# An interleaved state-space and feed-forward kernel: weight scales, a convolution step and a spectrum put elsewhere in a hand-ordered stretch

## The chip, the cores and the metric

The kernel runs on one core of a Trainium2 chip. A core has TensorE (PE in the profile), with a second queue for loading its weights (PEld), VectorE (DVE), ScalarE (ACT), GpSimd (POOL) and SyncE (SP), which here only issues transfers. Each engine works through its own list of instructions in order; engines wait for each other by semaphores. The metric is the device time of one execution, in microseconds (us).

## What is computed

Two rounds of two layers on a sequence `x` of 2048 rows and 512 channels: a state-space convolution and a gated feed-forward part, each behind a layer norm and with a residual. The core of the reference:

```python
dt = jnp.exp(log_dt)[:, None]
logdA, dB = dt * (A_re + 1j * A_im), dt * (B_re + 1j * B_im)
P = jnp.exp(logdA[:, :, None] * l[None, None, :])      # l = 0 .. 2047, 128 states
K = jnp.einsum("dn,dnl,dn->dl", Cc, P, dB).real
Kf, Uf = rfft2(pad(K)), rfft2(pad(u.T))
y = irfft2(Uf * Kf)[..., :L].T + u * Dskip

x = A_u
x = x + A_ref(layernorm(x), ...)      # the convolution above
x = x + B_ref(layernorm(x), ...)      # (silu(x @ w_gate) * (x @ w_up)) @ w_down, 1376 wide
x = x + A_ref(layernorm(x), ...)
x = x + B_ref(layernorm(x), ...)
```

Both rounds use the same weights and the same kernel `K`.

## The kernel before

**Tiling.** The sequence is cut into four blocks of 512 rows. The convolution is done block by block with short Fourier transforms, written as matmuls: the 512 rows fall into residues, called `q`, taken in the order 0, 3, 1, 2 (`QORD`), and the channels into two halves `h` of 256. A block's spectra are products of a DFT matrix with its normed rows (`direct`, L288 to L300, in fp32, to a DRAM buffer `udr`). One *step* of a convolution (`ssm_half`, L738) belongs to one `h` and `q`: for each of the blocks up to this one a product of its spectrum with the matching piece of the kernel's spectrum (L781; `w0r` stays in on-chip memory and serves the block itself, `wdr` holds the pieces for earlier blocks in DRAM), a sum (L784), two instructions that make the complex result `yf` (L786 and L787), and then the inverse transform on TensorE (L803, result `pi`) that ACT or DVE joins to sums and differences `bb` (L753, L761, L762). After the four steps of an `h`, some sixteen small instructions (from L818) add the outcome to the rows.

**Stages.** For the first 250 us or so the kernel's spectrum is generated in eight chunks of channels (`lags`, L496 and L497, then spectra, L531, L580). Weights are meanwhile loaded only to find their maxima, `cmx` (L339). From the maxima `scales` (L342 to L356, eleven tiny DVE instructions) makes powers of two, `sc`. With these each weight is split into a high half on ACT (L664) and a low half on DVE (L669), both fp16, `wsl`. From about 326 us the rest runs: (layer, block) in the order of `SEQ` = (0,0), (0,1), (0,2), (1,0), (0,3), (1,1), (1,2), (1,3), a feed-forward part for each (`ffn`: L916 to L919 into `pgu`, `sg` on ACT and DVE, L931 to L933 into `py`, the residual at L936), with the next block's convolution woven in.

**What lies between: the handoff**, about 250 to 326 us, is what the change touches. On PE, DVE, ACT and POOL it is written out by hand: within `manual_schedule` the order of the calls in the source is the order of the engines. `take(g, n)` runs the generator `g` through `n` of its yields; `split(hi, lo, load)` issues so many high halves, low halves and loads of weights. The work there is the eighth chunk's lags and spectra (`first_parts` L580, `later_parts` L531, with `wos` L598 to L600), block 0's convolution in two halves `conv[0]` and `conv[1]` (its spectra lie in `u4`, part of the tile `mix`, which is loaded again for the second half), the splitting of the first weights, block 0's second norm `norm` (statistics L203 to L209, `nn` L848, transposes L850, then L853 and L855 into `mix`), and the first steps of block 1's convolution, `block1`. `direct_size` (L187) takes the largest skip weight: `da` on ACT (L192), one row of 512, and `dmax` on DVE (L193). SP's list is ordered by a scheduler, and its transfers wait there in that order, each for its buffer.

**Buffers that matter.** Tile `uu` has three buffers, two of which hold the normed rows of block 1's neighbour whose last spectra are still to be taken (L296, `n`); `w` has three, `hf` and `y1` one, and there are four small accumulators (`pi`, `pw`, `pf`).

## Time and profile before

| | us |
|---|---|
| median of 3 runs | 1154.03 |
| lowest, highest | 1152.23, 1155.5 |
| the profiled execution | 1154.49 |
| its span | 1152.7 |
| PE busy in it | 1099.8 (95%) |
| DVE busy | 998.9 (87%) |
| ACT busy | 599.1 (52%) |
| POOL busy | 108.7 (9%) |

The profile is of one execution. Its views give groups of instructions by line and engine, the idle time before them with what ended it, the waits summed by line and by what was waited for, and a timeline. A row like `wsl<-st,sc` reads output from inputs; `[5.16 <-ACT wsl L664]` behind it says that the engine was idle for 5.16 us, until ACT's write of `wsl` at line 664. A transfer's time runs from its issue to its landing.

Line numbers are those of the kernel before. In the changed kernel the lines of `ssm_half` and what follows are others: L775 is the inverse transform (L803 before), L803 the product (L781), L806 the sum (L784), L808 and L809 make `yf` (L786, L787), L759 and L760 the `bb` on DVE (L761, L762), L751 the `bb` on ACT (L753), L864, L866, L869, L871 the norm's (L848, L850, L853, L855), L932, L933, L935 the gate and up products (L916, L917, L919), L939 `sg` (L923).

### The profile page before, as it was taken

The page shows a single profiled execution, that of the slowest core. Times are in us where ns is not written, and L with a number is a line of the kernel's source. Part 1 is how long each engine was busy: PE and PEld are TensorE (multiplying, and loading weights), DVE is VectorE, ACT ScalarE, POOL GpSimd, SP SyncE. Part 2 cuts the span into 40 slices and gives each one's busy share as a digit, 9 for nine tenths or more (in the row PEclk, how much of TensorE's full clock was granted, in tenths as well). Part 3 has the DMA queues.
Part 4 walks back from the last instruction along what each step waited for, and adds up shares of the span by engine and source line. Part 5 has one row for each costly group of instructions (what it writes and reads, how often), then busy time and mean ns, then how long its engine had stood idle before and what let it go on. Part 6 is the DMA issues. An engine that isn't in the chain of part 4 may idle for free.

```text
span 1152.7 us, 24401 instructions
## 1 busy us (share of the span) xinstructions
PE 1099.8 (95%) x9942; PEld 877.3 (76%) x9942; DVE 998.9 (87%) x1585; ACT 599.1 (52%) x1198; POOL 108.7 (9%) x163
## 2 busy tenths in 40 slices
PE   2989999998899999999999999999999999999998
PEld 1868888887876868686868687877778687876874
DVE  8999999988999899998999999989994999973211
ACT  6989889733554453567453534655434352334211
POOL 0112222210000010011010000110000100000000
PEclk9989999998999999999999999999999999999999
DMA  5367677867583355322353444333443155302000
GB/s 210 129 164 166 162 186 170 194 184 250 172 263 109 106 152 192 114 97 71 110 144 130 131 142 151 108 118 110 143 132 130 50 134 156 102 32 48 14 24 19
DMA packets 127314, 150.38 MB, mean 130 GB/s; under 512 B 50897, under 2 KB 75985, under 8 KB 127202
## 3 DMA queue, kind: packets, MB, share of 16 engines
q1 hardware_dynamic: 115298, 123.32, 34.6%
q0 software_dynamic: 11904, 25.50, 9.5%
q8 instruction: 78, 1.28, 0.5%
q14 instruction: 34, 0.28, 0.1%
HBM read 98.70 MB, written 33.82 MB: 115 GB/s over the span
## 4 chain that ended last, share of the span: by engine, by line
PE 40%; DVE 21%; issue 7%; ACT 3%; DMA 3%; POOL 1%; SPq 1%; DVEq 0%; ACTq 0%; POOLq 0%
PE pgu L916 7%; PE pgu L917 7%; PE pgu L919 7%; PE py L931 4%; PE py L932 4%; PE py L933 4%; PE pi L803 4%; DVE t L781 3%; DVE yk L784 3%; PE pf L280 2%; DVE z L228 2%; DVE yk L781 2%; DMA mix<-nn 1%; DVE sg L923 1%; DVE hl L925 1%
## 5 line engine op out<-in xcount | busy, mean ns | idle before, releaser
L916 PE MATMUL pgu<-mix,wsl 128*128 128x256 f16 x1280 | 299.4, 273 | 4.1 <-DVE sg L923 2.9
L917 PE MATMUL pgu<-mix,wsl 128*128 128x256 f16 x1280 | 299.1, 273 | 0.0
L919 PE MATMUL pgu<-mix,wsl 128*128 128x256 f16 x1280 | 195.6, 273 | 0.0
L917 PEld LDWEIGHTS <-wsl 128*128 128x128 f16 x1280 | 125.5, 98 | 20.9 <-issue 4.6
L931 PE MATMUL py<-wsl,hh 128*128 128x512 f16 (+1 forms) x352 | 133.4, 379 | 4.8 <-DVE xg L936 3.2
L916 PEld LDWEIGHTS <-wsl 128*128 128x128 f16 x1280 | 125.4, 98 | 16.1
L919 PEld LDWEIGHTS <-wsl 128*128 128x128 f16 x1280 | 125.6, 98 | 15.2
L933 PE MATMUL py<-wsl,hl 128*128 128x512 f16 (+1 forms) x352 | 133.4, 379 | 0.1
L922 ACT ACTIVATE sg<-pgu,sc 128x512 f32<-128x512 f32 x80 | 54.6, 683 | 128.4 <-PE pgu L919 126.6
L932 PE MATMUL py<-wsl,hh 128*128 128x512 f16 x320 | 121.3, 379 | 0.0
L781 DVE TENSOR_TENSOR t<-uu,w 128x1024 f32<-128x1024 f32 x96 | 116.8, 1216 | 0.2
L784 DVE TENSOR_TENSOR yk<-yk,t 128x1024 f32<-128x1024 f32 x96 | 116.7, 1216 | 0.2
L923 DVE SCALAR_TENSOR_TENSOR sg<-pgu,sc,sg 128x512 f32<-128x512 f32 x80 | 59.6, 745 | 52.6 <-ACT sg L922 52.3
L531 PE MATMUL pw<-kt,ek 128*128 128x256 f32 (+1 forms) x384 | 92.8, 380 | 0.0
L924 ACT ACTIVATE hh<-sg 128x512 f16<-128x512 f32 x80 | 50.1, 627 | 78.2 <-DVE sg L923 78.2
L531 PEld LDWEIGHTS pw<-kt,ek 128*128 128x128 f32 x384 | 74.3, 198 | 8.7
L803 PE MATMUL pi<-yl,mix 128*128 128x256 f16 x576 | 78.9, 273 | 1.2 <-ACT yl L792 0.8
L280 PE MATMUL pf<-z,eh 128*128 128x256 f16 x576 | 74.9, 273 | 0.6 <-DVE z L228 0.6
L781 DVE TENSOR_TENSOR yk<-u,w0r 128x1024 f32<-128x1024 f32 x56 | 68.1, 1216 | 0.8 <-ACT u L282 0.8
L925 DVE TENSOR_TENSOR hl<-sg,hh 128x512 f16<-128x512 f32 x80 | 54.8, 685 | 15.6 <-ACT hh L924 15.4
L496 PE MATMUL pk<-re,g 128*32 128x64 f32 x1024 | 65.1, 317 | 1.9 <-DMA g<-g 1.2
L932 PEld LDWEIGHTS <-hh 128*128 128x128 f16 (+1 forms) x352 | 34.5, 98 | 41.7 <-issue 5.9
(238 smaller groups left out, 2158.8 us busy)
## 6 DMA issues: line engine op xcount, KB each, us to landing
uu<-udr SPq DMA_DIRECT2D x96, 256.0 KB, 3.0
w<-wdr SPq DMA_DIRECT2D x96, 256.0 KB, 2.7
udr<-u POOLq DMA_DIRECT2D x32, 256.0 KB, 2.7
g<-g POOLq DMA_DIRECT2D x6, 1024.0 KB, 9.0
udr<-u SPq DMA_DIRECT2D x16, 256.0 KB, 2.9
n<-xdr SPq DMA_DIRECT2D x4, 1024.0 KB, 5.7
kdr<-ks SPq DMA_DIRECT2D x6, 512.0 KB, 2.6
kt<-kdr SPq DMA_DIRECT2D x24, 128.0 KB, 3.0
```

What stands on the lines that cost most here:

```text
L280: PE.matmul(pf[:, o], lhsT=e, rhs=m, start=k == 0, stop=k == len(terms) - 1)
L531: PE.matmul(pw[:, i], lhsT=e, rhs=kt[:, :, c + 4 * k0:4 * k1:4, :].rearrange("p g k d -> p k g d"), start=c == 0, stop=c == 3)
L781: V.tensor_tensor(t, uu.unsqueeze(2).to_broadcast([P, NQ, 2, 2, DC]), w.unsqueeze(3).to_broadcast([P, NQ, 2, 2, DC]), OP.mult)
L784: V.tensor_tensor(yk, yk, t, OP.add)
L803: PE.matmul(pi[:, o], lhsT=e, rhs=m, start=k == 0, stop=k == len(terms) - 1)
L916: PE.matmul(o, lhsT=wgu(wi, k, 0)[:, fs], rhs=nh[:, k], start=k == 0, stop=False)
L917: PE.matmul(o, lhsT=wgu(wi, k, 1)[:, fs], rhs=nh[:, k], start=False, stop=False)
L919: PE.matmul(o, lhsT=wgu(wi, k, 0)[:, fs], rhs=nlo[:, k], start=False, stop=k == 3)
L923: V.scalar_tensor_tensor(sg, pgu[:, 1], sc6[:, 4:5], sg, OP.mult, OP.mult)
L931: PE.matmul(py[:, r], lhsT=hh[:n, f, rc], rhs=wd(f, 0)[:n], start=f == 0, stop=False)
L932: PE.matmul(py[:, r], lhsT=hh[:n, f, rc], rhs=wd(f, 1)[:n], start=False, stop=False)
L933: PE.matmul(py[:, r], lhsT=hl[:n, f, rc], rhs=wd(f, 0)[:n], start=False, stop=f == FT - 1)
```

## The change

Three groups of steps change their place in the handoff; what is computed is the same.

1. The last weight maxima, the scales and the first high half stand right behind the eighth chunk's lags, ahead of everything of block 0's convolution. Its low half and a load follow sooner.
2. Block 1's first step (up to `yf`, without its inverse transform) stands ahead of block 0's second half, and with it `direct_size`; the second step stands where the first stood. Their inverse transforms are issued later, from a list (`made`, `inverse`). The first step's `u` is loaded in `ssm_half` itself, and its `yf` goes to a buffer of `w`.
3. The last spectrum of the second block (`second(*sec[-1])`: PE at L296, ACT at L299, a transfer to `udr`) stands ahead of the norm's transposes, in place of the end of the handoff; two of `later_parts`'s steps (`odd`) follow sooner too.

```diff
@@ inputs
+                        elif h + i == 0:
+                            continue
@@ ssm_half
-        if (layer, b) == SEQ[1] and not yf2:
-            t = tl([P, 2, 2, HD], "yf2", "hf")
-            yf2.extend((t[:, 0], t[:, 1]))
...
-        late = []
+        late, made = [], []
+        ahead_two = (layer, b, h) == (0, 1, 0)
+
+        def inverse(q, y, yl):
...
         for s in range(4):
-            hq, q, u = ahead.pop(0)
-            nxt = next(spec, None)
-            if nxt:
-                ahead.append(nxt)
+            if ahead_two and s == 0:
+                q, u = QORD[0], tl([P, NQ, 2, DC], "u", "u")
+                nc.sync.dma_start(u, udr[0][1, 0, q])
+            else:
+                hq, q, u = ahead.pop(0)
...
-            y = yc if half else yf2[s % 2] if (layer, b) == SEQ[1] else tl([P, 2, HD], "yf", "w")
+            if (layer, b, h + s > 0) == (*SEQ[1], True) and not yf2:
+                t = tl([P, 2, 2, HD], "yf2", "hf")
+                yf2.extend((t[:, 0], t[:, 1]))
+            y = yc if half else yf2[s % 2] if (layer, b, h + s > 0) == (*SEQ[1], True) else tl([P, 2, HD], "yf", "w")
...
-            if (layer, b, h, s) == (0, 1, 0, 0):
-                yield
...
+            made.append((q, y, yl))
+            if ahead_two and s == 0:
+                yield
+                continue
+            while made:
+                if ahead_two and s == 1:
+                    yield
+                inverse(*made.pop(0))
             yield
@@ weights: the last group's maxima are left for the handoff
-                    t0, t1, t2, t3 = 15.0, 20.0, 24.0, 27.0
+                    t0, t1, t2, t3 = 15.0, 20.0, 24.0, None
@@ the handoff
+        while tops:
+            tops.pop(0)()
+        scales()
+        split(1, 0)
         ks = spread_in(pk)
...
+        last = second(*sec[-1])
         norm = first_norm(tl([P, 2, D], "nn1", "hf"))
         take(conv[0], 1)
         spread_pe(ks, kts[1])
         skip(c, kts[1], G)
+        split(0, 1)
+        split(0, 0, 1)
         take(conv[0], 1)
-        scales()
-        split(1, 0)
         first_parts(c, 0)
         take(conv[0], 1)
-        split(1, 1)
-        split(0, 0, 1)
+        split(1, 0)
         first_parts(c - 1, 3)
         split(1, 0)
         take(conv[0], 1)
         first_parts(c - 1, 1)
         split(1, 0)
+        direct_size()
+        block1 = ssm(0, 1)
+        take(block1, 1)
+        split(0, 1)
+        split(0, 0, 1)
         take(conv[1], 1)
         first_parts(c, 2)
         take(conv[1], 1)
-        split(0, 1)
-        split(0, 0, 1)
...
-        direct_size()
-        block1 = ssm(0, 1)
         take(norm, 1)
         take(rest, 2)
         take(odd, 1)
+        take(last, 1)
+        take(odd, 2)
         take(norm, 1)
+        take(last, 1)
         take(block1, 1)
         take(rest, 1)
-        take(odd, 2)
         split(1, 0)
...
-        take(second(*sec[-1]), 2)
```

**DVE, from block 0's fourth step on, before.** `mix,w0r` are products of block 0, `u,w0r` and `uu,w` those of block 1.

```order
L781 TENSOR_TENSOR yk<-mix,w0r 128x1024
L786 TENSOR_TENSOR yf<-yk 128x256
L787 TENSOR_TENSOR yf<-yk 128x256
L761 TENSOR_TENSOR bb<-bb,pi 128x512
L762 TENSOR_TENSOR bb<-bb,pi 128x512
L781 TENSOR_TENSOR yk<-mix,w0r 128x1024
L786 TENSOR_TENSOR yf<-yk 128x256
L787 TENSOR_TENSOR yf<-yk 128x256
```

The same place now:

```order
L759 TENSOR_TENSOR bb<-bb,pi 128x512
L760 TENSOR_TENSOR bb<-bb,pi 128x512
L193 TENSOR_REDUCE dmax<-da 1x1
L803 TENSOR_TENSOR yk<-u,w0r 128x1024
L803 TENSOR_TENSOR t<-uu,w 128x1024
L806 TENSOR_TENSOR yk<-yk,t 128x1024
L808 TENSOR_TENSOR yf<-yk 128x256
L809 TENSOR_TENSOR yf<-yk 128x256
L669 SCALAR_TENSOR_TENSOR wsl_2666<-wsl_2667,sc_92,wsl_2665 128x4x344
L803 TENSOR_TENSOR yk<-mix,w0r 128x1024
```

`dmax`, the five instructions of block 1's first step and a low half stand between block 0's first `bb` pair and its fifth step.

**ACT, from the eighth chunk's lags on, before.** `ks<-pk` (L507) copies the lags.

```order
L507 ACTIVATE ks<-pk 128x1024
L753 ACTIVATE bb<-pi 128x512
L525 ACTIVATE kt_429<-kp 128x1024
L664 ACTIVATE wsl_2665<-st_2533,sc_92 128x4x344
L581 ACTIVATE w0r<-pw 128x128
L753 ACTIVATE bb<-pi 128x512
L664 ACTIVATE wsl_2666<-wsl_2668,sc_92 128x4x344
L581 ACTIVATE w0r<-pw 128x2x2x64
L664 ACTIVATE wsl_2665<-wsl_2668,sc_92 128x4x344
L581 ACTIVATE w0r<-pw 128x2x2x64
L664 ACTIVATE wsl_2666<-wsl_2668,sc_92 128x4x344
L753 ACTIVATE bb_2675<-pi 128x512
```

The same place now:

```order
L664 ACTIVATE wsl_2664<-st_2532,sc_92 128x4x344
L507 ACTIVATE ks<-pk 128x1024
L751 ACTIVATE bb<-pi 128x512
L525 ACTIVATE kt_429<-kp 128x1024
L581 ACTIVATE w0r<-pw 128x128
L751 ACTIVATE bb<-pi 128x512
L664 ACTIVATE wsl_2665<-wsl_2667,sc_92 128x4x344
L581 ACTIVATE w0r<-pw 128x2x2x64
L664 ACTIVATE wsl_2664<-wsl_2667,sc_92 128x4x344
L581 ACTIVATE w0r<-pw 128x2x2x64
L664 ACTIVATE wsl_2665<-wsl_2667,sc_92 128x4x344
L192 ACTIVATE da<-tdk 1x512
```

The first high half went ahead of the lags' copy, and `da` came up to right behind the fourth high half (before, it stood behind the fifth).

**PE, around the norm's transposes (`pt`), before**: products `pw` on either side, the spectrum's `pf` only behind eight of the products that follow.

```order
L531 MATMUL pw<-kt_429,ef 128x192
L531 MATMUL pw<-kt_429,ek_83 128x192 x3
L531 MATMUL pw<-kt_429,ef 128x192
L531 MATMUL pw<-kt_429,ek_83 128x192 x3
L850 MATMUL pt<-ident,nn_2676 128x128 x8
L531 MATMUL pw<-kt_429,ef 128x192
L531 MATMUL pw<-kt_429,ek_83 128x192 x3
```

The same place now, up to the first gate product `pgu`:

```order
L296 MATMUL pf<-n_1626,ef 128x256
L296 MATMUL pf<-n_1626,ek_84 128x256
L296 MATMUL pf<-n_1628,ek_84 128x256 x2
L531 MATMUL pw<-kt_429,ef 128x192
L531 MATMUL pw<-kt_429,ek_83 128x192 x3
L531 MATMUL pw<-kt_429,ef 128x192
L531 MATMUL pw<-kt_429,ek_83 128x192 x3
L866 MATMUL pt<-ident,nn_2691 128x128 x8
L531 MATMUL pw<-kt_429,ef 128x192
L531 MATMUL pw<-kt_429,ek_84 128x192 x3
L531 MATMUL pw<-kt_429,ef 128x192
L531 MATMUL pw<-kt_429,ek_84 128x192 x3
```

The spectrum and two products went ahead of the transposes; two products are left between these and `pgu`, where eight stood before, with the spectrum and an inverse transform.

More of the change, by code (lines that the diff above doesn't have):

```diff
@@ L787, in ssm_half @@
             V.tensor_tensor(yo[:, 1], yk[:, :, 0, 1], yk[:, :, 1, 0], OP.add)
-            if (layer, b, h, s) == (0, 1, 0, 0):
-                yield
+            yl = None
             if half:
@@ L793, in ssm_half @@
                 stt(yl[:, 1], y, sy[:, 0:1], yl[:, 0], OP.subtract)
-            pi = psml([P, 2, HD], "pi")
-            with tc.high_priority(offset=0 if first else BOOST):
-                for o in range(2):
-                    if half:
-                        terms = [(eih[:, q, 0 if i == o else 1 + o, le], yl[:, ly, i])
-                                 for i in range(2) for le, ly in ((0, 0), (0, 1), (1, 0))]
-                    else:
-                        terms = [(ei[:, q, 0 if i == o else 1 + o], y[:, i]) for i in range(2)]
-                    for k, (e, m) in enumerate(terms):
-                        PE.matmul(pi[:, o], lhsT=e, rhs=m, start=k == 0, stop=k == len(terms) - 1)
-            late.append((q, pi))
-            if first and q < 2 or len(late) > 1:
-                combine(*late.pop(-1 if first and q < 2 else 0))
+            made.append((q, y, yl))
[6 more added lines that the diff above has]
+                inverse(*made.pop(0))
             yield
@@ L1097, in weights @@
             at(t2, product)
-            at(t3, largest)
+            if t3:
+                at(t3, largest)
         starts = [0.0, 31.0, 62.0] + [93.0 + 28.0 * k for k in range(NCH)]
@@ L1111 @@
                 if i == NCH - 2 and k == 2:
-                    t0, t1, t2, t3 = 15.0, 20.0, 24.0, 27.0
+                    t0, t1, t2, t3 = 15.0, 20.0, 24.0, None
                 if n:
-                    weights(n, t + t0, t + t1, t + t2, t + t3)
+                    weights(n, t + t0, t + t1, t + t2, t3 and t + t3)
         t = starts[NCH - 1]
```

16 lines of the change are left out of this document (added).

## The prediction, made before the changed kernel ran

> **What bounds the kernel now.** I read the windows by stage first, to find where TensorE (PE) is not yet full. Columns: window, its length, then busy time of PE, its weight loads, VectorE (DVE), ScalarE (ACT), GpSimd (POOL), the granted TensorE clock, the DMA share, GB/s.
>
> ```profile
> 282.00:290.00 8.00, 7.07 (x28) 6.38 (x29) 6.93 (x13) 2.79 (x7) 0.00 (x0) 0.68 0.76 237
> 326.00:400.00 74.00, 72.45 (x586) 57.19 (x586) 67.93 (x123) 29.16 (x59) 2.62 (x5) 0.98 0.44 132
> 400.00:1000.00 600.00, 592.82 (x5022) 462.13 (x5021) 567.76 (x942) 287.82 (x559) 49.01 (x59) 1.00 0.41 125
> 1000.00:1152.00 152.00, 146.92 (x1173) 106.56 (x1171) 57.75 (x88) 37.39 (x68) 1.83 (x5) 1.00 0.11 31
> ```
>
> From 326 to the end PE works 812 of 826 us. The change takes no matmul away there, so whatever PE loses or gains in the handoff (about 250 to 330) stays to the end. DVE is the second engine: it is idle 6 of 74 us from 326 to 400, so it can't catch up much before the first feed-forward parts are through. Next, the waits: engine, waiting line, what it waited for, us in total, times, longest. The first four rows and the sixth are of 250 to 326, the fifth of 326 to the end.
>
> ```profile
> PE pi L803 <- DVE yf L786: 3.9, 2, 2.7
> PE pt L850 <- ACT nn L848: 3.6, 1, 3.6
> ```
> ```profile
> DVE wsl L669 <- ACT wsl L664: 5.2, 1, 5.2
> ...
> DVE bb L761 <- PE pi L803: 0.8, 1, 0.8
> DVE mix L600 <- ACT mix L599: 0.7, 1, 0.7
> ```
> ```profile
> PE pgu L916 <- DVE sg L923: 2.9, 2, 2.7
> ```
>
> PE loses 3.9 + 3.6 = 7.5 us to the inverse transforms of block 0's second half and to the norm's transposes, and 2.7 more in the first feed-forward part, all three for DVE or for ACT behind DVE. DVE's one large loss is the 5.2 us at the first low half, for ACT's first high half. So the change aims at the right places; the question is what it puts ahead of what.
>
> **The change, part by part.** Times are the start and the duration in us, of the one profiled execution.
>
> Scales and first high half. DVE rows:
>
> ```profile
> 250.03 1.21 DVE L781 TENSOR_TENSOR yk<-mix,w0r 128x1024 f32<-128x1024 f32 x1
> ...
> 254.06 0.16 DVE L344 TENSOR_REDUCE c<-cmx 128x3 f32<-128x6 f32 x1
> ...
> 255.72 1.22 DVE L781 TENSOR_TENSOR yk<-mix,w0r 128x1024 f32<-128x1024 f32 x1
> ...
> 262.90 1.78 DVE L669 SCALAR_TENSOR_TENSOR wsl<-st,sc,wsl 128x688 f16<-128x688 f32 x2 [5.16 <-ACT wsl L664]
> ...
> 266.59 0.68 DVE L761 TENSOR_TENSOR bb<-bb,pi 128x512 f32<-128x512 f32 x1
> ...
> 272.03 1.65 DVE L669 SCALAR_TENSOR_TENSOR wsl<-wsl,sc,wsl 128x1376 f16<-128x1376 f32 x1
> ```
>
> The eleven scale instructions take 255.72 - 254.06 = 1.66. They now stand first: 250.03 to 251.7. The high half (1.43 by the ACT rows below) then falls into the idle time of ACT that ends at 256.81, and its low half finds it done: the 5.2 us are gone. Two steps of block 0 take 254.06 - 250.03 = 4.03, so four take 8.06; with 1.78 for the low half DVE stands at 250.03 + 1.66 + 8.06 + 1.78 = 261.5 before the first subtraction and sum (`bb`), which wait for the second inverse transform. That one is unchanged on PE, which works through without a gap:
>
> ```profile
> 260.37 1.99 PE L803 MATMUL pi<-yf,mix 128*128 128x256 f32 x8
> ...
> 271.02 1.89 PE L803 MATMUL pi<-yf,mix 128*128 128x256 f32 x8
> ```
>
> It ends at 262.3; two `bb` of 0.66 bring DVE to 263.6. This part alone would let DVE go on 4.3 us earlier than the 267.91 at which it began block 0's fifth step before; but PE is busy until the fifth inverse transform at 271.02 whatever DVE does.
>
> Block 1's first step in front of block 0's second half. What stands on DVE ahead of it is `dmax`, which needs `da` from ACT, and ACT's queue has the fourth high half ahead of `da`:
>
> ```profile
> 256.81 1.02 ACT L507 ACTIVATE ks<-pk 128x1024 f32<-128x1024 f32 x1 [7.71 <-PE pk L497]
> ...
> 271.22 0.38 ACT L581 ACTIVATE w0r<-pw 128x256 f32<-128x256 f32 x1 [1.77 <-PE pw L580]
> 271.50 1.43 ACT L664 ACTIVATE wsl<-wsl,sc 128x1376 f16<-128x1376 f32 x1
> ...
> 283.66 0.61 ACT L192 ACTIVATE da<-tdk 1x512 f32<-1x512 f32 x1
> ...
> 294.89 1.52 ACT L848 ACTIVATE nn<-xg,rs 128x512 f32<-128x512 f32 x2 [4.68 <-DVE rs L209]
> ```
>
> The copy at 271.22 waits for PE's product, and PE is where it was. So `da` runs from 272.9 to 273.5, and DVE, free at 263.6, stands for 273.5 - 263.6 = **9.9 us** behind an instruction of one row. Everything that PE needs next is queued there. The costs that follow are those of these rows:
>
> ```profile
> 290.63 0.67 DVE L193 TENSOR_REDUCE dmax<-da 1x1 f32<-1x512 f32 x1
> ...
> 295.24 1.21 DVE L781 TENSOR_TENSOR yk<-u,w0r 128x1024 f32<-128x1024 f32 x1
> 296.38 1.22 DVE L781 TENSOR_TENSOR t<-uu,w 128x1024 f32<-128x1024 f32 x1
> ...
> 298.99 0.43 DVE L786 TENSOR_TENSOR yf<-yk 128x256 f32<-128x256 f32 x1
> ```
>
> `dmax` 0.6, block 1's first step 4.4 (295.24 to the end of the second `yf`, which follows the one at 298.99), the low half of 1.6 that stands next, and 1.9 for block 0's fifth step: its inverse transform starts at 273.5 + 0.6 + 4.4 + 1.6 + 1.9 = 282.0 in place of 271.02. **PE stands 11.0 us.**
>
> Its loads: `w` for this step is issued on SyncE's queue behind the last reloads of `u`, the last of which went out here:
>
> ```profile
> 265.84 0.34 SPq L713 DMA_DIRECT2D mix<-udr  x1
> ```
> ```profile
> uu<-udr SPq DMA_DIRECT2D x5, 256.0 KB, 7.0
> w<-wdr SPq DMA_DIRECT2D x5, 256.0 KB, 4.3
> ```
> ```profile
> mix<-udr SPq DMA_DIRECT2D x2, 256.0 KB, 9.8
> ```
>
> (256 KB loads, median us to landing: two kinds between 225 and 330, the third between 255 and 275.) At 4.3 `w` is there at 270.5, hidden under the 9.9; at 9.8 it comes at 276.0 and adds 2.5. I take nothing, because the ordinary case is covered.
>
> Up to the second step. DVE loses 9.9 and saves 5.2 + 0.8 (the `bb` wait: PE is no longer behind DVE there): 3.9 late, and it has block 1's first step done besides. So what stood behind that step's place comes 3.9 + 4.4 = 8.3 later in time: the eighth inverse transform, which waited for DVE, at 291.2, the norm's first `nn` at 303.2, the product with `uu` of block 1's second step, standing where the first stood, at 304.7. PE rows:
>
> ```profile
> 282.93 3.75 PE L803 MATMUL pi<-yf,mix 128*128 128x256 f32 x8 [1.14 <-DVE yf L786]
> 286.47 0.84 PE L531 MATMUL pw<-kt,ef 128*128 128x192 f32 x2
> ...
> 288.13 0.49 PE L531 MATMUL pw<-kt,ef 128*128 128x192 f32 x2
> ...
> 289.43 0.49 PE L531 MATMUL pw<-kt,ef 128*128 128x192 f32 x2
> ...
> 295.76 1.36 PE L850 MATMUL pt<-ident,nn 128*128 128x128 f32 x8 [3.57 <-ACT nn L848]
> ```
>
> Behind the eighth inverse transform PE now has four spectrum products of 1.3 each (288.13 to 289.43), the moved last spectrum (sixteen records like two inverse transforms of 1.75: 3.5) and two more products, 11.3 in all, before the transposes. It ends at 293.1 (or 294.7 at the slow rate of the row at 282.93), so the transposes start at 304.4 to 306.0. `nn` is there by 304.1: the 3.6 us wait is filled, as intended.
>
> The second step's `uu` has its load behind that spectrum, since the buffers it needs hold the block that the spectrum reads; this is what is late next. They come free at 301.8 to 303.4, take 302.6. With 0.4 to issue and a landing of 7.0 (the row of this stretch; 9.8 at worst by the `mix` row), the data is there at 310.0, and DVE waits 5.3. The page's row for the whole span is the other bound:
>
> ```profile
> uu<-udr SPq DMA_DIRECT2D x96, 256.0 KB, 3.0
> ```
>
> With 3.0 DVE waits 1.3, with 9.8 it waits 8.1. Before, the product standing here (296.38) shows no wait, so this one is new. I take 7.0, since the moved block has the same reloads and weights in flight.
>
> Behind that step stand two sums of spectra and the sum of the transposed norm, which is the first feed-forward part's input:
>
> ```profile
> L600 DVE TENSOR_TENSOR wos<-pw,wos 128x384 f32<-128x384 f32 x4 | 2.2, 549 | 0.0
> ...
> L855 DVE TENSOR_TENSOR mix<-pt,mix 128x1024 f16<-128x1024 f32 x1 | 1.2, 1214 | 0.0
> ```
>
> The remainder of the step is 3.3, the sums 1.1, the last 1.2: input ready at 310.0 + 5.6 = 315.6. PE has the transposes (1.2) and only two products (2.6) to fill that time: before, eight products, a spectrum and an inverse transform stood between. It is out of work at 305.2 + 3.8 = 309.0 and **waits 6.6 us** (2.6 at the low bound, 9.4 at the high one).
>
> The sum, twice. PE's waits: 11.0 + 6.6 in place of 7.5: 10.1 later (6.1 to 12.9). DVE: 9.9 + 5.3 less 5.2, 0.8 and the 0.7 behind `mix`: 8.5 later (4.5 to 11.3). The first feed-forward part waits for DVE already (2.7), so DVE's lateness isn't hidden there; and a part of PE's can be won back only where DVE had been the later one. I take 9, between the two. The profiled execution took 1154.49 us, 1.8 more than its span and within 0.5 of the median of the runs (1154.03): 1154.5 + 9 = **1163.5 us**. Both accounts together give 1159 to 1167 as this case's own range.
>
> The clock. After the waits of 2.73 and 1.14 us the window 282 to 290 was granted 0.68, and eight records took 3.75 instead of 1.89: short waits already cost PE about 2.6 us in the trace, which are taken to recur behind the 11.0. [...]
>
> That a wait of one tiny operand holds all of DVE up is the row at 262.90: 5.16 us behind ACT with independent steps queued behind. [...]
>
> **The rivals.** (1) Loads worse than that: `w` at 276 (2.5) and `uu` at the high bound (2.8), and the weights' later loads behind them: 9 + 5.3, about 1169. For it: the landing of 9.8 in just this stretch. Against it: both must happen. Chance 0.10. (2) The delay is absorbed: the first step's 4.4 and the filled 3.6 give back most of the 9.9, and `uu` lands in 3.0. DVE is then 4.5 late at the first feed-forward part, and the 6 us of DVE's idle time from 326 to 400 take 2 to 4 of these: about 1156. For it: PE has products that could be put in the gaps. Against it: in the order they stand behind the waiting ones. Chance 0.14. (3) Faster: block 1's first step runs in DVE's free time from 263.6 to 270, that is, `dmax` doesn't wait. Then the 5.2 and PE's 7.5 are gone, less the `uu` wait of 2 to 3: about 1149. It decides itself at `da`: if ACT has it by 266, this case holds. For it: `da` takes 0.6, needs only a row of constants, and ACT is idle 1.77 before 271.22. Against it: it stands behind a copy that waits for PE until 271.22. Chance 0.10. That the change doesn't do what its words say is a part of this forecast: the step reaches the first wait's place, but not its time.
>
> **The numbers.** The forecast has 0.66. About 0.3% (3.5 us) is what a measurement here can tell from no change. Slower: 0.66 + 0.10 = 0.76; same: 0.14; faster: 0.10. A range of 8 in 10 takes in the forecast's 0.66 and, beyond its ends, the upper part of the second case and the lower part of the first: 1156.5 to 1168; the faster case stays outside.
>
> **What would show it.** Right: `dmax` on DVE at 273 to 274 with a wait of some 10 us for ACT; the fifth inverse transform at about 282 with 11 us of PE's wait; no wait at the transposes; the second step's product waiting for its `uu` load; the first feed-forward matmul waiting at some 309 to 316. Wrong: `dmax` before 266, the fifth inverse transform still near 271, or PE with less than 10 us of waits in the handoff. If these waits are there and the end is nevertheless where it was, the claim that PE can't win the time back after 326 is the step that failed.

## The result, and the profile after

The changed kernel takes 1173.45 us (median of 4 runs, 1171.93 to 1174.94), the kernel before 1154.26 in the same comparison: a ratio of 1.0171, 95% interval 1.0157 to 1.0186, **19 us slower**. The prediction was 1163.5, range 1156.5 to 1168. The sign held, the size did not.

TensorE's busy row after, of the page:

```profile
PE 1102.0 (94%) x9942; PEld 879.3 (75%) x9942; DVE 999.2 (85%) x1585; ACT 599.4 (51%) x1198; POOL 113.6 (10%) x163
```

The span went from 1152.7 to 1171.7. PE's busy time rose by 2.2 (1099.8 to 1102.0) and its idle time by 16.8 (52.9 to 69.7): 19.0 together. So the loss is in PE's waits, and they can be counted. In the rows of the changed kernel L952 is the residual (L936 before), L947 to L949 make `py` (L931 to L933), and L899 is a gate product of the last 96 columns. First the waits of the handoff, 250 to 345, PE then DVE (as before: who waited for whom, us in total, times, longest):

```profile
PE pi L775 <- DVE yf L808: 12.1, 1, 12.1
PE pw L531 <- DVE wos L600: 2.5, 1, 2.5
PE pgu L932 <- DVE sg L939: 1.7, 1, 1.7
```
```profile
DVE dmax L193 <- ACT da L192: 9.6, 1, 9.6
DVE t L803 <- DMA uu<-udr: 6.6, 1, 6.6
...
DVE t L803 <- issue: 1.3, 1, 1.3
```

The DVE timeline at the first wait, and PE's around it:

```profile
263.19 0.69 DVE L760 TENSOR_TENSOR bb<-bb,pi 128x512 f32<-128x512 f32 x1
273.46 0.67 DVE L193 TENSOR_REDUCE dmax<-da 1x1 f32<-1x512 f32 x1 [9.59 <-ACT da L192]
274.07 1.20 DVE L803 TENSOR_TENSOR yk<-u,w0r 128x1024 f32<-128x1024 f32 x1
276.60 1.23 DVE L803 TENSOR_TENSOR t<-uu,w 128x1024 f32<-128x1024 f32 x1 [1.33 <-issue]
```
```profile
283.23 3.78 PE L775 MATMUL pi<-yf,mix 128*128 128x256 f32 x8 [12.06 <-DVE yf L808]
...
307.89 1.04 PE L866 MATMUL pt<-ident,nn 128*128 128x128 f32 x8
...
311.36 0.27 PE L932 MATMUL pgu<-mix,wsl 128*128 128x256 f16 x1
...
317.45 0.59 PE L531 MATMUL pw<-kt,ef 128*128 128x192 f32 x2 [2.45 <-DVE wos L600]
```

The waits of 5.2 on DVE and 3.6 at the transposes are gone, as the change wants. In their place DVE stands 9.6 us before `dmax`, and PE 12.1 at the fifth inverse transform. PE's waits up to 345 sum to 16.3, against 3.9 + 3.6 + 2.7 = 10.2 before: 6.1 more. That leaves 10.7 of the 16.8 to be found behind the handoff. The waits of PE from 345 to 378, the first feed-forward part, where the kernel before has none:

```profile
PE pgu L932 <- DVE sg L939: 4.1, 1, 4.1
PE pgu L899 <- DVE sg L939: 2.7, 1, 2.7
```

These are 6.8. DVE stands late there with work that it had behind it before: low halves of `w_down` (L692), right in front of `sg`:

```profile
349.13 2.07 DVE L692 SCALAR_TENSOR_TENSOR wsl<-st,sc,wsl 128x512 f16<-128x512 f32 x3
351.12 0.74 DVE L939 SCALAR_TENSOR_TENSOR sg<-pgu,sc,sg 128x512 f32<-128x512 f32 x1
```

In the kernel before all eleven are done by 326. They depend on loads; SyncE issues the last two at 311.00 before; after, the last one stands behind loads of `u` that wait for DVE's products, and leaves at 335.16:

```profile
323.63 2.07 DVE L692 SCALAR_TENSOR_TENSOR wsl<-st,sc,wsl 128x512 f16<-128x512 f32 x3
```
```profile
311.00 0.93 SPq L683 DMA_DIRECT2D st<-in_B_w_down_dram  x2
```
```profile
334.79 0.32 SPq L718 DMA_DIRECT2D u<-udr  x1
335.16 0.43 SPq L683 DMA_DIRECT2D st<-in_B_w_down_dram  x1
```

DVE doesn't stand for these loads (its waits between 318 and 352 are 0.6 us in all): the low halves come later in its list, and it does them when `sg` is due. In the six kernels of the table below that have the spectrum early (the first two, scales_and_spectrum, no_da_late_rows, both_steps_late, low_later_spectrum), the last of these loads leaves 12 to 13 us behind the one before it; in all others the two are at most 4.4 us apart.

The rest of the idle time, about 4, is further on. The largest piece is a wait of 4.46 at 616, where the next product needs the accumulator that DVE's residual frees; the residual stands on DVE behind products of another block's convolution, though the matmuls that it reads are done at about 611.5:

```profile
615.58 0.74 DVE L952 SCALAR_TENSOR_TENSOR xf<-py,sc,xf 128x512 f32<-128x512 f32 x1
```
```profile
616.38 0.27 PE L932 MATMUL pgu<-mix,wsl 128*128 128x256 f16 x1 [4.46 <-DVE xf L952]
```

To tell these places apart in the runs below, each is compared with the kernel before at two rows of DVE: the second residual (the end of the first feed-forward part; L936, 374.12 before) and the last one (1148.27 before). "Handoff" is the lateness at the first, "end" at the last. Rows of before, then of after:

```profile
374.12 0.75 DVE L936 SCALAR_TENSOR_TENSOR xg<-py,sc,xg 128x512 f32<-128x512 f32 x1 [1.91 <-PE py L933]
...
1148.27 0.75 DVE L936 SCALAR_TENSOR_TENSOR xg<-py,sc,xg 128x512 f32<-128x512 f32 x1 [7.38 <-PE py L933]
```
```profile
387.79 0.75 DVE L952 SCALAR_TENSOR_TENSOR xg<-py,sc,xg 128x512 f32<-128x512 f32 x1 [0.48 <-PE py L949]
...
1167.45 0.75 DVE L952 SCALAR_TENSOR_TENSOR xg<-py,sc,xg 128x512 f32<-128x512 f32 x1 [7.38 <-PE py L949]
```

The changed kernel is 13.7 late at the first and 19.2 at the last: 5.5 are lost behind the first feed-forward part. Behind these residuals PE is idle 4.4 us more than before and busy 0.9 more, with nearly as many matmuls (6,420 and 6,416 records).

| run | median us | ratio to before (95%) | handoff | end |
|---|---|---|---|---|
| changed kernel | 1173.45 | 1.0157 to 1.0186 | +13.7 | +19.2 |
| da_early | 1171.74 | 1.0138 to 1.0172 | +12.9 | +17.8 |
| delay_only | 1167.43 | 1.0105 to 1.0137 | +11.5 | +11.6 |
| scales_only | 1159.10 | 1.0033 to 1.0063 | +4.2 | +3.7 |
| scales_and_spectrum | 1159.21 | 1.0033 to 1.0063 | +4.2 | +4.8 |
| scales_late_rows | 1154.09 | 0.9987 to 1.0011 | -1.9 | -1.9 |
| scales_low_later | 1152.50 | 0.9976 to 0.9998 | -1.3 | -1.5 |
| no_da_late_rows | 1170.01 | 1.0116 to 1.0183 | +8.4 | +14.2 |
| no_spectrum | 1169.23 | 1.0108 to 1.0151 | +8.1 | +14.0 |
| both_steps_late | 1169.58 | 1.0137 to 1.0174 | +11.1 | +15.4 |
| two_steps_only | 1156.47 | 1.0019 to 1.0046 | +0.9 | +1.1 |
| low_later_spectrum | 1155.72 | 1.0006 to 1.0041 | +0.9 | +3.2 |
| low_later_products | 1152.68 | 0.998 to 1.0 | -4.8 | -1.9 |
| one_product_a | 1151.37 | 0.9972 to 0.9991 | -1.2 | -0.5 |
| one_product_b | 1151.45 | 0.997 to 0.9992 | -2.5 | -3.5 |

Medians and ratios are of the timed runs; the lateness is of each kernel's one profiled execution, and executions of a kernel differ by 1 to 2 us.

### The profile page after: what moved, and what is told of

Read it like the earlier page. It is cut to its first block, busy times and chain, and to the rows that moved or that the text cites. A ratio compares the mean times of both kernels' runs of the same rounds, so it can differ in the third digit from the quotient of the medians.

```text
span 1171.7 us, 24407 instructions
## 1 busy us (share of the span) xinstructions
PE 1102.0 (94%) x9942; PEld 879.3 (75%) x9942; DVE 999.2 (85%) x1585; ACT 599.4 (51%) x1198; POOL 113.6 (10%) x163
## 4 chain that ended last, share of the span: by engine, by line
PE 40%; DVE 21%; issue 6%; ACT 3%; DMA 3%; POOL 1%; SPq 1%; DVEq 0%; ACTq 0%; POOLq 0%
PE pgu L932 7%; PE pgu L933 7%; PE pgu L935 7%; PE py L947 4%; PE py L948 4%; PE py L949 4%; PE pi L775 3%; PE pf L280 3%; DVE t L803 3%; DVE yk L806 2%; DVE z L228 2%; DVE yk L803 2%; DMA mix<-nn 2%; POOL rs L223 1%; DVE sg L939 1%
## 5 line engine op out<-in xcount | busy, mean ns | idle before, releaser
L933 PE MATMUL pgu<-mix,wsl 128*128 128x256 f16 x1280 | 301.1, 274 | 0.0
L935 PE MATMUL pgu<-mix,wsl 128*128 128x256 f16 x1280 | 197.0, 274 | 0.0
L933 PEld LDWEIGHTS <-wsl 128*128 128x128 f16 x1280 | 125.9, 98 | 27.4 <-issue 11.1
L947 PE MATMUL py<-wsl,hh 128*128 128x512 f16 (+1 forms) x352 | 133.5, 379 | 6.6 <-DVE xg L952 5.8
L935 PEld LDWEIGHTS <-wsl 128*128 128x128 f16 x1280 | 125.8, 98 | 15.6
L949 PE MATMUL py<-wsl,hl 128*128 128x512 f16 (+1 forms) x352 | 133.4, 379 | 0.0
L282 ACT ACTIVATE u<-pf 128x512 f32<-128x512 f32 x48 | 28.4, 592 | 80.6 <-PE pf L280 80.6
```

The lines of the kernel that those rows point to most:

```text
L933: PE.matmul(o, lhsT=wgu(wi, k, 1)[:, fs], rhs=nh[:, k], start=False, stop=False)
L935: PE.matmul(o, lhsT=wgu(wi, k, 0)[:, fs], rhs=nlo[:, k], start=False, stop=k == 3)
L947: PE.matmul(py[:, r], lhsT=hh[:n, f, rc], rhs=wd(f, 0)[:n], start=f == 0, stop=False)
L949: PE.matmul(py[:, r], lhsT=hl[:n, f, rc], rhs=wd(f, 0)[:n], start=False, stop=f == FT - 1)
```

## The experiments

**da_early.** Is it `dmax` that holds the step?

```diff
         scales()
         split(1, 0)
+        direct_size()
...
-        direct_size()
         block1 = ssm(0, 1)
```

> The changed kernel with the skip weight's size (da on ACT, dmax on DVE) put right behind the scales, far ahead of block 1's first step; everything behind the handoff keeps the changed kernel's order. Theory A, of the prediction: dmax's wait for da (9.6 us in the changed kernel) is what holds the fifth inverse transform; without it DVE goes on at 264, block 1's first step is done by 269 and TensorE's wait of 12.1 shrinks to 2 or less: 8 to 10 us faster than the changed kernel, about 1164. Theory B: the load of w for the same step, issued at 265.8 behind three reloads on a full DMA, lands at about 276.5 and would have been waited for anyway: DVE's wait moves from dmax to the product with uu and is about 11 us, TensorE's wait stays at 11 to 13, the time stays within 2 us of the changed kernel's 1173.

1171.74, within 2 us of the changed kernel: theory B, though the wait at the product is 8.4 and not 11. DVE's waits from 250 to 345:

```profile
DVE t L803 <- issue: 8.4, 1, 8.4
DVE t L803 <- DMA uu<-udr: 5.4, 1, 5.4
DVE dmax L193 <- ACT da L192: 3.2, 1, 3.2
```

The wait went from `dmax` to the product with `uu` and `w`. "issue" means that the profile shows no releaser; that it is the load of `w` is concluded from no_da_late_rows below, where the same wait has its name. (Here DVE's product starts at 276.90. In the changed kernel it starts at 276.60, behind a DMA that moves 389 GB/s from 270 to 272, 373 from 272 to 274 and 27 from 275 to 276.) `dmax` still waits 3.2 us at its new place: by the program `da` and `wo` take turns in one buffer, so `da` has to wait for the transfer `wdr<-wo` (in the changed kernel two of these, issued from 250.13 on, landed 2.3 to 4.1 us after their issue; that this is the wait here is argued), and DVE reaches the step at 267.3 in place of 264; the wait for `w` would have covered that too. This load was the second gate behind `dmax`, hidden in the changed kernel but for 1.3 us.

**delay_only.** What does a stall of that size cost by itself?

```diff
-                V.tensor_tensor(t, ..., OP.mult)
+                for _ in range(12 if (layer, b, h, s) == (0, 0, 1, 0) else 1):
+                    V.tensor_tensor(t, ..., OP.mult)
```

> The kernel before with one product of block 0's fifth step (the first of its second half) done twelve times in place of once, the same result each time: 11 more products of about 1.2 us on DVE in front of the fifth inverse transform, 13 us of work, and nothing else; the order of all engines behind the handoff is that of the kernel before. DVE had about 1 us to spare there, so TensorE stands some 11 to 12 us, as in the changed kernel. Theory A: such a delay goes to the end one for one or less, 8 to 13 us slower than before, and the rest of the changed kernel's 19 us has another cause, behind the handoff. Theory B: the 19 us all follow from the delay in the handoff (slow clock, DVE late in the feed-forward part): 16 to 20 us slower.

1167.43, 13 us slower; theory A. PE's waits in the handoff:

```profile
PE pi L804 <- DVE yf L787: 15.9, 3, 12.3
PE pt L851 <- ACT nn L849: 4.8, 1, 4.8
```

PE stands 12.3 us at the fifth inverse transform, as in the changed kernel, and the residuals show what becomes of it (lines from L781 on are one higher in this kernel):

```profile
385.66 0.75 DVE L937 SCALAR_TENSOR_TENSOR xg<-py,sc,xg 128x512 f32<-128x512 f32 x1 [0.71 <-PE py L934]
...
1159.86 0.75 DVE L937 SCALAR_TENSOR_TENSOR xg<-py,sc,xg 128x512 f32<-128x512 f32 x1 [7.38 <-PE py L934]
```

11.5 late at the first feed-forward part's end, 11.6 at the last residual: with the old order behind the handoff, nothing is added and nothing won back.

**scales_only** and **scales_and_spectrum.** The parts without block 1's early step.

```diff
+        while tops:
+            tops.pop(0)()
+        scales()
+        split(1, 0)
         ks = spread_in(pk)
...
+        split(0, 1)
+        split(0, 0, 1)
         take(conv[0], 1)
-        scales()
-        split(1, 0)
```

> The kernel before with the first part of the change alone: the last maxima, the scales and the first high half right behind the lags; the order behind the handoff is that of the kernel before. Theory A: DVE's wait of 5.2 us goes and DVE is some 4 us ahead from the fifth step on, so TensorE's waits of 2.7 and 1.1 for the inverse transforms go, and the transposes come up to 4 us sooner: 3 to 7 us faster than before, 1147 to 1151. Rival: TensorE is the bound up to 271 and the transposes then wait for something else, so that it is within 2 us of before.

> The kernel before with the first and the third part of the change: scales first, and the last spectrum ahead of the transposes; block 1's first step stays where it was. Theory A: as with the first part alone, and the spectrum's 3.5 us and two products fill the transposes' wait: 4 to 9 us faster than before. Rival: the spectrum ahead delays what it was put ahead of (the loads of uu for block 1 need its buffers), and the order behind the handoff, which is another one here, costs several us: not faster than the first part alone, or slower than before.

1159.10 and 1159.21, about 5 us slower than before: theory A misses in both, and of the rivals only the second one's holds (not faster than the first part alone). Moving the scales costs time by itself. DVE in scales_only:

```profile
274.24 1.23 DVE L781 TENSOR_TENSOR yk<-mix,w0r 128x1024 f32<-128x1024 f32 x1 [7.80 <-DMA mix<-udr]
```

DVE is early for its sixth step and waits for the reloaded spectra. The reloads' issue, before and in scales_only:

```profile
251.27 2.42 SPq L713 DMA_DIRECT2D mix<-udr  x2
```
```profile
262.85 2.63 SPq L713 DMA_DIRECT2D mix<-udr  x3
```

A reload may go out when the product that reads the old spectra is done. Before, two steps ran ahead of the scales (their products end at 251.24 and 253.33) and two reloads left at 251 to 254, ahead of the block's rows and the weights, which are issued from 256.75 on; the DMA moved 238 GB/s from 256.7 to 262 and 381 from 262 to 268. With the scales and a low half ahead, only one goes out in time; the scheduler puts the others behind the rows and the weights (two loads of 1024 KB and four of 688). With the spectrum early as well, the transposes' wait goes, but DVE waits 6.5 us for `uu`, and PE for `wos` and `sg`: it is as late at the second residual as without.

**scales_late_rows, scales_low_later.** Less in front of the reloads, then the steps sooner.

```diff
         take(conv[1], 1)
         first_parts(c, 2)
         take(conv[1], 1)
+        V.memset(xs[1][:, 0, :1], 0.0)
```

and for the second also the low half behind block 0's third step:

```diff
-        split(0, 1)
-        split(0, 0, 1)
         take(conv[0], 1)
         first_parts(c, 0)
         take(conv[0], 1)
-        split(1, 0)
+        split(1, 1)
+        split(0, 0, 1)
```

> The kernel before with the first part of the change, and block 1's rows (the second of the two 1 MB loads xg, needed only some 50 us later) held back until block 0's sixth step by a tiny write to their buffer; three of the four reloads of block 0's spectra then go out ahead of it. Theory A: what made the first part alone 4.7 us slower are these reloads, which the earlier scales put behind the large loads on SyncE's queue (DVE waits 7.8 us for mix<-udr, TensorE 5.3 for DVE); with 1 MB less ahead (2.7 us at 385 GB/s) that wait falls to 5 or less and the time to 1153 to 1156. Theory B: the loss comes from elsewhere (the transposes' wait of 4.7, a feed-forward part): within 1.5 us of 1159.

> As the run before it, and the first low half behind block 0's third step in place of ahead of its second, so that the steps that free the spectra's buffers come sooner and two reloads go out ahead of the next weights. Theory A (the reloads set the pace): DVE's wait for mix<-udr falls under 2 us, TensorE's waits for the inverse transforms to under 3, and the first part's 4 us on DVE are seen: 1146 to 1151, faster than before. Theory B: within 1.5 us of 1159, or of before at best.

1154.09 and 1152.50: 5 and 6.6 us faster than scales_only, as theory A has it for the first; the second falls short of the 1151 hoped for. DVE's wait for `mix` goes from 7.8 to 4.0 and 2.2. So the reloads are what made the first part slow. What it gives when they are mended is 0.1% (interval 0.02 to 0.24%), under the 0.3% that a measurement here can tell: PE still waits 3.1 and 4.9 at the inverse transforms and the transposes.

**no_da_late_rows.** The changed kernel with both gates of the step eased: `direct_size` ahead of the scales, block 1's rows held back, and the low half later (edits as above).

> The changed kernel with da and dmax ahead of the scales (no wait for them at all), block 1's rows held back and the first low half behind the third step: the load of w for block 1's first step has some 1.7 MB less in front of it. Theory A: the step's place is set by that load, which now lands 3 to 5 us sooner (271 to 273); DVE waits 5 to 8 us at the product with uu, TensorE 7 to 9 for the fifth inverse transform: 3 to 6 us faster than the changed kernel, 1166 to 1170, and still well slower than before. Theory B: with dmax and the rows away the step runs in DVE's free time: TensorE's wait under 3, about 1160.

1170.01, 3.4 us faster than the changed kernel: theory A, at the weak end.

```profile
267.94 1.22 DVE L803 TENSOR_TENSOR yk<-u,w0r 128x1024 f32<-128x1024 f32 x1
273.06 1.23 DVE L803 TENSOR_TENSOR t<-uu,w 128x1024 f32<-128x1024 f32 x1 [3.91 <-DMA w<-wdr]
```

Here the wait has its name. PE's waits for inverse transforms are 9.0 in four pieces. The step takes 4.4 us of DVE's time, and the room for it between 264 and 270 isn't there: `dmax` still waits 3.9 us for `da`, so that DVE comes to the step at 267.94, and `w` isn't there before 273.

**no_spectrum.** The changed kernel with the last spectrum at the handoff's end.

```diff
-        take(last, 1)
-        take(odd, 2)
         take(norm, 1)
-        take(last, 1)
         take(block1, 1)
         take(rest, 1)
+        take(odd, 2)
...
+        take(second(*sec[-1]), 2)
```

> The changed kernel without its third part (the last spectrum at the handoff's end, as before). Theory A: the handoff's loss is that of the second part: TensorE's wait of 12 us at the fifth inverse transform stays, the uu wait of 6.6 at the second step goes, and the transposes wait some 3 to 5 again, so that it comes out within 3 us of the changed kernel as far as the first feed-forward part's end (some 12 us behind before); what follows depends on the order that the scheduler takes behind the handoff. Theory B: the spectrum's place (its buffers, and the load of uu behind them) is a large part: 5 us or more faster than the changed kernel.

1169.23, between the two theories: the handoff is 5.6 us shorter (+8.1 in place of +13.7). PE stands 11.9 at the fifth inverse transform as before and 4.3 at the transposes again, but the `uu` wait is gone, the last `w_down` loads go out at 321.0 together, and there is no wait for `sg` from 345 to 378. So the third part, meant to fill 3.6 us, cost more than that here: it delays `uu` (DVE waits 5.3 to 6.6 us for it in each of the six kernels with the spectrum early, at most 0.8 in the others), with it the `u` loads that wait for DVE's products, and the weights queued behind those on SyncE:

```profile
321.00 0.93 SPq L683 DMA_DIRECT2D st<-in_B_w_down_dram  x2
```

The order behind the handoff is another one again here, far from that of both kernels, so the end (+14.0) is not the spectrum's place alone.

**both_steps_late** and **two_steps_only.** Is the loss behind the first feed-forward part a consequence of the stall, or of the order that the scheduler then takes?

```diff
-        direct_size()
-        block1 = ssm(0, 1)
-        take(block1, 1)
...
+        direct_size()
+        block1 = ssm(0, 1)
         take(norm, 1)
...
+        take(block1, 1)
         take(block1, 1)
```

> The changed kernel with block 1's first step (and da, dmax) not in front of block 0's second half but right in front of the second step: TensorE has no 12 us stall at the fifth inverse transform, and the order that the scheduler takes behind the handoff is nearly that of the changed kernel (32 of some 1,070 DVE rows differ, all near its start). Lateness is counted at the first feed-forward part's residuals (at 374 us in the kernel before) and at the end. Theory A: some 6 us of the changed kernel's 19 are the price of that order and not of the stall: whatever this kernel's lateness is at the first residuals (I expect 3 to 9), the end is 4 to 8 later still: 1161 to 1171. Theory B: the later loss is a consequence of the stall: the end is as late as the first residuals, within 2 us.

> The kernel before with the changed kernel's code for the first steps of block 1, both of them in the handoff at the place where the first one was, without the scales' move and the spectrum's; the order behind the handoff is nearly that of the kernel before (67 DVE rows differ). Theory A: the order behind the handoff decides about the later 6 us, so here the end is as late as the first residuals, within 2 us; the handoff itself has one step of 4.4 us more on DVE ahead of the first feed-forward part: 0 to 6 us slower than before. Theory B: two steps in the handoff, wherever they stand, cost the later 6 us by themselves: the end at least 4 us later than the first residuals.

both_steps_late keeps the changed kernel's order behind the handoff and has no 12 us stall:

```profile
385.26 0.75 DVE L952 SCALAR_TENSOR_TENSOR xg<-py,sc,xg 128x512 f32<-128x512 f32 x1
...
1163.65 0.75 DVE L952 SCALAR_TENSOR_TENSOR xg<-py,sc,xg 128x512 f32<-128x512 f32 x1 [7.38 <-PE py L949]
```

It is 11.1 late at the first row, more than the 3 to 9 expected (PE waits 7.7 for DVE's `wos` behind a `uu` wait of 5.9), and 15.4 at the last: 4.2 lost behind, and its waits from 378 on name the same 4 us at the same line:

```profile
PE pgu L932 <- DVE xf L952: 4.1, 1, 4.1
```

two_steps_only has both steps in the handoff too, with nearly the old order: +0.9 and +1.1. So both runs, with delay_only, speak for theory A: the later loss goes with the order and not with the stall.

**low_later_spectrum** and **low_later_products.** Can the transposes' wait be filled? To scales_low_later, the first adds the spectrum ahead of the transposes, the second only two products:

```diff
         take(odd, 1)
+        take(odd, 2)
         take(norm, 1)
         take(block1, 1)
         take(rest, 1)
-        take(odd, 2)
```

> The run with the scales first, the low half later and block 1's rows held back (1152.5 us), and the last spectrum ahead of the transposes. Theory A: the transposes' wait of 4.9 us is filled, and the time falls to 1147 to 1150. Theory B: the load of uu for block 1's first step comes behind the spectrum, whose rows hold its buffer, DVE waits some 6 us for it as in the changed kernel (6.6) and the gain is given back: 1151 to 1156.

> The run with the scales first, the low half later and block 1's rows held back (1152.5 us), and the two products that stood behind the transposes put ahead of them, without the spectrum, so that no load of uu comes later. Theory A: they fill 2.6 of the transposes' 4.9 us, and the time is 1149 to 1151. Theory B: TensorE has less to do behind the transposes and waits there or at the first feed-forward part for DVE, or the order behind the handoff, which is another one again (235 DVE rows), takes the gain: 1152 to 1156.

1155.72 and 1152.68: theory B twice. In the first DVE waits for `uu` as it did in the changed kernel:

```profile
DVE t L781 <- DMA uu<-udr: 5.3, 1, 5.3
```

The second is 4.8 early at the second residual and only 1.9 at the last, under yet another order.

**one_product_a** and **one_product_b.** The same once more, one product ahead, in two ways that leave the old order behind the handoff.

```diff
-        take(odd, 1)
+        take(odd, 2)
+        take(rest, 1)
         take(norm, 1)
         take(block1, 1)
-        take(rest, 1)
-        take(odd, 2)
+        take(odd, 1)
```

(b; a leaves `take(rest, 1)` behind `block1`.)

> To scales_low_later, one product (1.3 us) put ahead of the transposes, such that the order behind the handoff stays that of the kernel before but for 9 DVE rows. low_later_products, with two products ahead, was 4.8 us early at the second residual and 1.9 at the last: 2.9 lost behind, under another order (235 rows). Theory A: that loss goes with the order; here the end is as early as the second residual, within 0.7 us: at 374 some 2 to 4 early, at the end too, 1150 to 1152. Theory B: what is won in the handoff is lost behind it whatever the order (DVE is the bound there): at least 1.5 of it lost by the end, 1152 to 1154.

> As one_product_a, with the next chunk's third step (its ACT copies and DVE's sum) ahead of the transposes as well; the same 9 DVE rows differ behind the handoff. The same two theories: A, at the end as early as at 374, 1150 to 1152; B, at least 1.5 of it lost by the end.

1151.37 and 1151.45. a goes from 1.2 early to 0.5, b from 2.5 to 3.5: within 1 us, a hair over the 0.7 named, and in both directions; neither loses the 1.5 of theory B. a's 1.2 is also less than the 2 to 4 expected at 374. These are the best versions found: 0.2% faster than the kernel before (intervals 0.1 to 0.3%, under the 0.3% named above) and 22 us faster than the changed one, with the scales first, the loads and the order seen to, and one product ahead of the transposes.

## Why the prediction was wrong in size

**The step that failed.** The forecast put two terms at nothing: work that DVE still has in the first feed-forward part beyond the handoff's lateness, and a new order behind the handoff ("whatever PE loses or gains in the handoff (about 250 to 330) stays to the end"). The runs showed 6.8 us of PE's waits for the first and 5.5 lost behind that part for the second. What it did count came out smaller than forecast: PE's waits in the handoff are 12.1 + 2.5 in place of 7.5, 7.1 more, against a forecast of 10.1.

**Right, by its own rows.** `dmax` at 273 to 274 with some 10 us of wait: 273.46, 9.59. The fifth inverse transform at 282.0 with 11.0: 283.23, 12.06. No wait at the transposes, at 304.4 to 306.0: none, at 307.89. DVE waiting 5.3 for `uu`: 6.57. The rival that made it faster had `da` as its point; da_early gives `da` early and shows that this would not have been enough.

**"At 4.3 `w` is there at 270.5, hidden."** It was hidden only because the forecast's own stall was longer: the product started at 276.60, 10.8 after the issue at 265.8. That it cost so little was luck. The rows with the bound were there (9.8 for the reloads in that stretch); the ordinary case chosen came from a window five times as long. (The forecast's 2.5 for that bound is wrong by its own rows: the step's first product needs no `w` and ends at 275.3, so `w` at 276.0 adds 0.7.) The cost beside `dmax` was 1.3, but the reading of the cause changes: the step had two gates, and taking the first away gains 1.7, no more than the intervals allow for chance.

**"PE is busy until the fifth inverse transform whatever DVE does", with the first part at no cost.** The part's effect on the reloads of `u` was not looked at. scales_only shows 5 us. In the changed kernel this is covered by the stall, so it isn't in the 19.

**"Waits 6.6 us" for the feed-forward's input.** This term was too large: the first gate products read only the high part of the normed rows, which ACT makes, done at 310.0, and ran from 311.36 without a wait; the products with DVE's low part come later (L935). PE waited 2.45 in between, for `wos`.

```profile
308.96 1.02 ACT L869 ACTIVATE mix<-pt 128x1024 f16<-128x1024 f32 x1 [2.02 <-PE pt L866]
```

Up to 345 PE waited 6.1 more than before (7.1 without the `sg` waits, which the forecast's 10.1 leaves out).

**"DVE's lateness isn't hidden there".** True, but sized as the lateness at the handoff. DVE's own queue was longer there: the eleven low halves of `w_down`, finished by 326 before, ran from 331 to 351; their last load had moved on SyncE's queue behind loads that wait for DVE. PE waited 6.8 for `sg`. no_spectrum, whose loads go out at 321, has no such wait, and neither has delay_only, which is nearly as late but has its loads at 324 together. That it is the loads that put the low halves there, and not the order by itself, is argued.

**The order behind the handoff** was the step left out. The forecast took it as unchanged ("whatever PE loses or gains in the handoff stays to the end"). The scheduler orders that part anew, and the changed order costs 5.5 us after the first feed-forward part (4.2 to 5.9 in the five kernels that have the early scales and two steps of block 1 in the handoff; 0.2 or less in delay_only and two_steps_only, which keep the old one; 2.9 and 2.3 in the two low_later runs with a third and a fourth order, against a change of at most 1.0 in the one_product runs with the old one). Another order need not cost that much: scales_and_spectrum, in which about as many rows of DVE move as in the low_later runs, loses 0.6. These runs agree that the loss goes with the order, but none changes the order alone; which of its many moved rows cost what is shown only for the 4.46 at 616. What stays open is why the scheduler takes it with both edits and not with one. A `dmax` put behind block 1's step, with `da` where it is, was not tried.

So the 16.8 of idle time are 6.1 in the handoff, 6.8 in the first feed-forward part, and some 4 behind it. The 2.2 of busy time, at the same number of matmuls, go with a slower clock (0.984 granted over the whole run, 0.990 before); where they arise was not worked out.

## What to carry to other kernels

An instruction moved into another engine's idle time brings its operands' loads along: find the landing time of each in the stretch where it will now be needed, on the queue as it will then be, before counting the idle time as free. Look also at the steps that it pushes back: what their end releases (here a buffer and its reload) comes later, and so do the loads queued behind it. And where a scheduler orders the rest, compare that order too: a local edit may cost as much far behind it as at its place, and a kernel with the stall alone and the old order tells the two apart.

## What the runs showed of the hardware

TensorE's granted clock was lower after the short waits of the kernel before too. After 12.06 us of waiting, in the changed kernel, it was 0.50 for the first 9 us of work, up to about 292.2, and 0.99 from there to 296 (columns as in the prediction's windows):

```profile
283.20:286.60 3.40, 3.37 (x8) 2.74 (x9) 3.30 (x6) 0.00 (x0) 0.00 (x0) 0.50 0.55 191
286.60:290.00 3.40, 3.40 (x17) 3.31 (x16) 3.26 (x8) 0.60 (x1) 0.00 (x0) 0.50 0.00 0
290.00:293.40 3.40, 3.40 (x13) 2.86 (x13) 3.30 (x6) 0.28 (x1) 0.00 (x0) 0.67 0.00 0
```

The work from 283.23 to 290.11 took 6.9 us in place of 3.5 (271.02 to 274.48 before), a loss of 3.4, and some 1 more behind it (the 24 records from 290.11 on took 6.69, three times 1.89 is 5.67). In the kernel before, the clock was 0.72 and 0.50 in the two windows that begin around the ends of waits of 2.73 and 1.14 us, at 279.15 and 282.93, and the work there took about 2.6 more (2.64 and 3.75 us for eight records in place of 1.89):

```profile
279.00:282.00 3.00, 2.64 (x8) 1.70 (x8) 3.00 (x5) 0.17 (x1) 0.00 (x0) 0.72 0.00 0
282.00:285.00 3.00, 2.07 (x5) 1.74 (x6) 2.86 (x6) 2.42 (x4) 0.00 (x0) 0.50 0.88 258
285.00:288.00 3.00, 3.00 (x12) 2.64 (x12) 2.18 (x3) 0.00 (x0) 0.00 (x0) 0.64 0.54 162
```

The prediction took these 2.6 to recur; here the loss was 3.4 and some 1 more.

Three reloads of 256 KB, issued behind the rows and weights at 262.95 to 265.5 in the changed kernel, took 10.8 us in the median, against 3.0 for the 96 loads `uu<-udr` of that size over the whole span. The product that needs `w` started 10.8 after its issue. The DMA moved 367 to 401 GB/s (slices of 0.45 us) from 262 up to about 274.

```profile
mix<-udr SPq DMA_DIRECT2D x3, 256.0 KB, 10.8
```

In no_da_late_rows, where 1 MB of rows was held back, `w` was issued at 266.48 and the product that waits for it by name started 6.6 later, at 273.06. The size of the load was the same each time; what stood in front was not: both loads of 1024 KB in the changed kernel, one here.
